# Float32 value path for four units, a fourth place for weight tiles, the first x's spread in other PSUM banks, and weight decoding queued behind its unit

## The chip, the cores and the metric

The kernel runs on one core of one Trainium2 chip. A core has five engines that run at the same time and are kept in step by semaphores: TensorE (PE in the profile, with its weight loads as PEld), VectorE (DVE), ScalarE (ACT), GpSimd (POOL) and SyncE (SP), which here issues every transfer. 16 DMA engines carry out the transfers. SBUF is the working memory and PSUM the small memory that matmuls write, in eight banks.

The metric is the device time of one execution, in microseconds (us). Each engine works off its instructions in a fixed order, one queue per engine, so an instruction that waits holds back those behind it.

## The reference

The inputs q, k and v have 4 batches, 8 heads, 768 positions and 64 columns; there are 16 centroids for each head. Every query and every key belongs to the centroid nearest in angle, and a query attends only to keys of its own cluster. The result goes through an MLP with a squared relu:

```python
q_assign = np.argmax(np.einsum('bhsd,hcd->bhsc', q_n, c_n), axis=-1)
k_assign = np.argmax(np.einsum('bhsd,hcd->bhsc', k_n, c_n), axis=-1)
mask = q_assign[:, :, :, None] == k_assign[:, :, None, :]
scores = np.where(mask, scale * np.matmul(q, k.transpose(0, 1, 3, 2)), -1e9)
attn = np.exp(scores - np.max(scores, axis=-1, keepdims=True))
attn = attn / (np.sum(attn, axis=-1, keepdims=True) + 1e-09)
x = np.matmul(attn, v).transpose(0, 2, 1, 3).reshape(B * S, H * D)
g = s * np.maximum(x @ w_in, 0.0) ** 2 + b
out = g @ w_out
```

w_in is 512 x 2048 and w_out 2048 x 512. Both lie in memory as 64-bit floats, so the kernel reads two 32-bit words for each weight and makes a float32 of them.

## The kernel before, in words

**Units.** The attention is cut into 192 units. A unit is one batch, one head and 128 queries (one of two column tiles t of a chunk of 256), against all 768 keys. They run in the order batch, chunk c (3), pair of heads hp (4), t, head h; so 16 units make one chunk of 256 rows of x, four units one pair of heads in it. A unit i passes these stages:

- `scores` (L456): four matmuls of 384 columns into a PSUM tile `sc`. The cluster mask is folded into the operands KA, KB, QA and QB, which `prep_k` and `prep_q` make from k and q: split into float16 high and low parts, transposed by DMA, matched to centroids by small matmuls (`pk`, `pq`) and a one-hot (L282).
- `maxima` (L470): a maximum over the row on DVE; `exps` (L477): a bias and the exponential on ACT, into `p`.
- `low` (L497): for the first 16 units (`TURN`) `p` is transposed on PE, in two halves e of three 128 x 128 blocks, into `turned`, one PSUM tile with two banks. For the first 8 units (`RAW`) each half is copied out as float32, half 0 by DVE and half 1 by ACT (L512, recorded at L122 and L120). For units 8 to 15 ACT copies each half as a float16 high part (L514) and DVE subtracts it to make the low part (L515). From unit 16 on the split stands before a DMA transpose (L519).
- `values` (L521): for units below 16, two at a time, the transposed weights times v. Below `RAW` that is 6 float32 matmuls a unit (L531, two records each) with v as it was loaded; else 18 float16 matmuls (L536 to L538) with the split `vh`, `vl` of v that `prep_v` makes (L407). Below `RAW` the row's sum comes from the exponential's accumulator, else from a column of ones in `vh`. From unit 16 on `value` (L551) does it in `sc`'s spare columns.
- `finish_x` (L577): after four units, the pair's part of x is split and transposed by DMA. After the fourth pair the largest value of the chunk is found across partitions by `allmax` (L94): a matmul spreads the columns, and DVE takes the maximum. `allmax` takes a one-bank PSUM tile, either of tag m or of tag h. Tag m has one buffer, which `px`, `pk`, `pq` and other spreads use in turn; tag h, also with one, belongs to the MLP's `h`.

**Weights.** The 32 weight tiles (16 of w_in, 16 of w_out, by turns) are loaded and decoded in the opening. `fetch` (L190) issues the load of one tile, 512 KB, into a stage of 4 KB per partition with three buffers (L198). `rebase` (ACT, L204) and `narrow` (two steps of DVE, L208 and L209) make the float32, and free the stage. `bound` (L212) finds the sums of absolute values, on ACT, and for w_in tiles with matmuls (L221) and a maximum on DVE (L222). After the last tile come the scales in `glob`; the column sums of w_out are spread by an `allmax` at tag m. `weights` (L228) is a generator that runs these with one tile between each two stages; three of its steps are traced before the main loop and two in each step of it (L785). When it is done, `wsplit` (L260) splits the tiles into float16 parts, on ACT (L266) and DVE (L268), one tile of each matrix from step 17 on.

**The MLP.** It has 192 steps of 256 rows x 128 hidden columns, and step m is traced with unit m + 21 (`LAG`). `mlp_start` (L602) makes the chunk's scales from the maximum of x with seven small DVE steps, `mlp_in` (L614) is 12 matmuls into `h` (L620), `mlp_relu` (L623) a relu with that scale and two squares on ACT (L627 to L630), `mlp_gl` a subtraction on POOL (L635) and `mlp_out` (L638) 6 matmuls into `acc` (L647), two steps later. `g` has four buffers of 1 KB per partition. `acc` and `turned` share one PSUM buffer of two banks (tag acc).

**The order.** The main loop (L746) traces units, MLP steps and background work step by step. The order on each engine is then made at build time, by a scheduler with a time model of its own: it issues what is ready in the model, and by priority among that. Work in a `high_priority` block is preferred; `first_of_all` (L689) gives it to the units below 20. `tc.issue_after`, wrapped as `behind` (L129), puts the instructions of a block behind a named instruction on that instruction's own engine, as an order and not as a wait. `load` puts the transfers behind the last transpose in that way.

Of the kernel before, what the change touches and what calls it, by code (L numbers as in the profile page):

```python
# [8 lines left out]
F16 = mybir.dt.float16  # L9
# [9 lines left out]
P = 128  # L19
# [7 lines left out]
def tile_cluster_attention_mlp(ctx, tc, q, k, v, cent, w_in, w_out, s_in, b_in, out):  # L27
# [15 lines left out]
    LAG = 21  # L43
    BIGN = 11

    RAW = 8
    TURN = 16
    URGENT = 20

# [43 lines left out]

    def allmax(dst, src, name, bank="m"):  # L94
        n = src.shape[1]
        pm = (ps_m if bank == "m" else ps_h).tile([P, 512], F32, tag=bank, name=f"am_{name}")
        for j in range(n):
            nc.tensor.matmul(pm[:, j * P : (j + 1) * P], src[:, j : j + 1].broadcast_to([P, P]), identb, start=True, stop=True)
        V.tensor_reduce(dst, pm[:, : n * P].rearrange("p (n q) -> p n q", q=P), axis=AX.X, op=ALU.max)
# [14 lines left out]
    G.tensor_copy(identb, ident)  # L114
    ones16 = const([P, P], F16, "ones16")
    G.memset(ones16, 1.0)

    def copy(eng, dst, src):
        if eng is A:
# [46 lines left out]
    wo = {}  # L166
    WSP = {}

    def weight_tile(name):
        return cp.tile([P, KT, P], F32, tag="w", name=name, bufs=2 * NF + 1)  # L170
    w1 = const([P, NF], F32, "w1")
# [18 lines left out]
    def fetch(p):  # L190
        ft = p // 2
        if p % 2 == 0:
            w = wi[ft] = weight_tile(f"wi{ft}")
            src = w_in.bitcast(I32)[:, ft * 2 * P : (ft + 1) * 2 * P].rearrange("(t p) f -> p t f", p=P)
        else:
            w = wo[ft] = weight_tile(f"wo{ft}")
            src = w_out.bitcast(I32)[ft * P : (ft + 1) * P, :].rearrange("p (a f) -> p a f", a=KT)
        st = sb.tile([P, KT, P, 2], I32, tag="stage", name=f"wst_{p}", bufs=3)  # L198
        load(st.rearrange("p a f w -> p a (f w)"), src)
        return {"w": w, "st": st, "p": p, "ft": ft}  # L200

# [25 lines left out]

    def weights():  # L228
        live = {}
        for i in range(2 * NF + 3):  # L230
            if 0 <= i - 3:
                bound(live[i - 3])
                narrowed[0] += 1
            if 0 <= i - 2 < 2 * NF:
                rebase(live[i - 2])
                narrow(live[i - 2])
            if i < 2 * NF:
                live[i] = fetch(i)
            if i < 2 * NF + 2:
                yield  # L240

    def finish_w_in():
# [164 lines left out]
    def prep_v(b):  # L407
        vm = sb.tile([P, 8], F32, tag="vm", name=f"vm_{b}", bufs=2)
        VM[b] = vm
        vns = []  # L410
        for hp in range(NP):
            vn = sb.tile([P, 2, T, D], F32, tag="kv", name=f"vn_{b}_{hp}", bufs=5)
            load(vn, v[b, 2 * hp : 2 * hp + 2].rearrange("h (p t) d -> p h t d", t=T), False)
            vns.append(vn)
            if b == 0:
                VN[hp] = vn
            yield
        if b:
            yield from until(START[b][3])
        for hp in range(NP):  # L420
            absmax(vm[:, hp : hp + 1], vns[hp].rearrange("p h t d -> p (h t d)"))
            if hp < NP - 1:
                yield
        vc = columns(1, f"v{b}")
        V.tensor_reduce(vc, vm[:, 0:NP], axis=AX.X, op=ALU.max)
        if b:
            yield
        allmax(vm[:, 5:6], vc, f"v{b}")
        yield
        floor2(V, vm[:, 6:7], vm[:, 5:6])  # L430
        inverse2(V, vm[:, 7:8], vm[:, 6:7], 0)
        V.tensor_scalar(vm[:, 7:8], vm[:, 7:8], 2.0 ** 13, None, op0=ALU.mult)
        V.tensor_scalar(vm[:, 6:7], vm[:, 6:7], 2.0 ** -19, None, op0=ALU.mult)
        for hp in range(NP):
            vh = sb.tile([P, 2, T, D + 2], F16, tag="vh", name=f"vh_{b}_{hp}", bufs=5)
            vl = sb.tile([P, 2, T, D], F16, tag="vl", name=f"vl_{b}_{hp}", bufs=5)
            VS[(b, hp)] = (vh, vl)
            G.memset(vh[:, :, :, D:], 1.0)
            yield from split(vh[:, :, :, :D], vl, vns[hp], vm[:, 7:8], False)
            if hp < NP - 1:  # L440
                yield
                if b > 0:
                    yield from until(48 * b - 8 + 4 * hp)
# [133 lines left out]
    def finish_x(g):  # L577
# [14 lines left out]
        if hp == NP - 1:  # L592
            xm = XM[(b, c)]
            xc = columns(1, f"x{g}")
            V.tensor_reduce(xc, xm[:, 0:NP], axis=AX.X, op=ALU.max)
            allmax(xm[:, 5:6], xc, f"x{g}")


    MS = {}
# [23 lines left out]
    def mlp_relu(b, c, ft):  # L623
# [1 line left out]
        ph = GS[(b, c, ft)]  # L625
        r = sb.tile([P, CW], F32, tag="r", name=f"r_{n}", bufs=2)
        A.activation(r, ph[:, :CW], AF.Relu, scale=MS[(b, c)][0])  # L627
        g = sb.tile([P, 2, CW], F16, tag="g", name=f"g_{n}", bufs=4)
        A.activation(g[:, 0, :], r, AF.Square)  # L629
        A.activation(r, r, AF.Square)  # L630
        GS[(b, c, ft)] = (r, g)
# [54 lines left out]
        at(LAG - 4 + ft, wsplit(ft))  # L686
    wgen = weights()

    def first_of_all(k):  # L689
        return tc.high_priority(offset=300) if k < URGENT else nullcontext()  # L690

    def run(gen):
        for _ in gen:
            pass
# [41 lines left out]
    with behind(last_turn[0], *last_split):  # L736
        some(first_v, 1)
        sv = scalar_in(s_in, "sv")
        bv = scalar_in(b_in, "bv")
        some(wgen, 3)  # L740
    run(first_k[0])
    run(first_q[0])
    run(first_k[1])
# [2 lines left out]
    while i < NU + 8 or i - LAG < NS + 4:  # L746
# [21 lines left out]
                exps(i)  # L768
        if 0 <= m < NS:
            if steps[m][2] == 0:  # L770
                mlp_start(*steps[m][:2])
            mlp_in(*steps[m])
            mlp_relu(*steps[m])
        if 0 <= i - 1 < NU:
# [38 lines left out]
```

## Time and profile before

| | |
|---|---|
| median of 3 runs | 953.33 us (951.72 to 954.87) |
| the profiled execution | 951.04 us |
| its span, from the first to the last instruction | 949.3 us |
| mean granted TensorE clock | 0.946 |
| read from HBM, written | 35.69 MB, 6.29 MB |

The profile is of one execution, and the difference between its time and its span is 1.7 us. In its 40 slices a digit is the busy share of a slice in tenths, and the granted clock in tenths of full speed. In lists of instructions, a number is the mean duration or the start, and brackets name what ended the engine's idle time. L-numbers are lines of the kernel before. A float32 matmul is recorded as two.

### The profile page before, as it was taken

What the parts mean: (1) busy time and instruction counts of PE and PEld (TensorE: products, weight loads), DVE (VectorE), ACT (ScalarE), POOL (GpSimd) and SP (SyncE); (2) the same over time, 40 slices, a digit from 0 to 9 for tenths busy, and PEclk for the clock granted to TensorE, in tenths of its full rate; (3) what the DMA queues carried; (4) which work ended last, traced back from release to release, by engine and by line L of the source; (5) the groups of instructions that cost most, each with busy time, mean ns of one, the idle gap of its engine ahead of it and who ended that gap; (6) DMA issues with size and microseconds to landing.
All of it is one profiled execution on the core that took longest, in us unless ns stands there. A gap on an engine that the chain in (4) does not pass through costs nothing. (4 is left out here: it accounts for less than half of the span.)

```text
span 949.3 us, 22900 instructions
## 1 busy us (share of the span) xinstructions
PE 835.3 (88%) x8673; PEld 586.3 (62%) x8673; DVE 639.7 (67%) x1680; ACT 713.9 (75%) x1406; POOL 546.4 (58%) x580
## 2 busy tenths in 40 slices
PE   0567566988999898999998999999999999999997
PEld 0356343656566566777676666666776667777664
DVE  7797888999577767667876766776686567654100
ACT  3476766777587777888887978887888788888443
POOL 3010114577576666778687667776776666676321
PEclk9967575899999899999999999999999999999999
DMA  6888813778787897969778877888978768575300
GB/s 174 219 215 242 225 38 78 181 141 145 160 157 146 178 200 132 181 150 180 157 173 151 198 181 147 160 146 185 180 160 167 145 129 165 125 161 114 46 23 23
DMA packets 437759, 144.25 MB, mean 152 GB/s; under 512 B 405392, under 2 KB 434064, under 8 KB 437648
## 3 DMA queue, kind: packets, MB, share of 16 engines
q1 hardware_dynamic: 437648, 142.78, 71.6%
q8 instruction: 68, 1.11, 0.5%
q14 instruction: 43, 0.35, 0.1%
HBM read 35.69 MB, written 6.29 MB: 44 GB/s over the span
## 5 line engine op out<-in xcount | busy, mean ns | idle before, releaser
L517 POOL TENSOR_TENSOR ph<-p,ph 128x768 f16<-128x768 f32 x176 | 298.5, 1696 | 92.8 <-ACT ph L120 53.8
L647 PE MATMUL acc<-wos,g 128*128 128x512 f16 x1152 | 299.8, 381 | 5.1 <-POOL g L635 4.6
L620 PE MATMUL h<-x,wis 128*128 128x256 f16 x2304 | 290.5, 275 | 5.1 <-DMA x<-xn 3.3
L620 PEld LDWEIGHTS <-wis 128*128 128x128 f16 x2304 | 220.5, 98 | 53.7 <-issue 6.7
L635 POOL TENSOR_TENSOR g<-r,g 128x256 f16<-128x256 f32 x192 | 135.0, 704 | 120.8 <-ACT r L630 100.7
L485 ACT ACTIVATE p<-sc,ssm,qsm 128x768 f32<-128x768 f32 x192 | 188.3, 981 | 2.1
L475 DVE TENSOR_REDUCE ssm<-sc 128x1 f32<-128x768 f32 x192 | 181.9, 948 | 6.9 <-PE sc L465 6.9
L647 PEld LDWEIGHTS <-g 128*128 128x128 f16 x1152 | 102.7, 98 | 82.3 <-POOL g L635 7.5
L627 ACT ACTIVATE r<-h,cf 128x256 f32<-128x256 f32 x192 | 89.6, 467 | 77.2 <-PE h L620 63.4
L120 ACT ACTIVATE ph<-p 128x768 f16<-128x768 f32 x164 | 136.4, 832 | 0.6
L482 ACT ACTIVATE ssm<-ssm,lift,qsm 128x1 f32<-128x1 f32 x192 | 73.0, 380 | 70.5 <-DVE ssm L475 68.9
L563 PE MATMUL sc<-vh,PT 128*128 128x65 f16 x1032 | 118.1, 196 | 7.0 <-DMA PT<-ph 6.8
L565 PE MATMUL sc<-vh,PT 128*128 128x65 f16 x1032 | 120.5, 194 | 0.0
L564 PE MATMUL sc<-vl,PT 128*128 128x64 f16 x1032 | 119.4, 193 | 0.0
L563 PEld LDWEIGHTS <-PT 128*128 128x128 f16 x1056 | 99.4, 98 | 26.4 <-DMA PT<-ph 13.7
L465 PE MATMUL sc<-KA,QA 128*128 128x384 f16 x384 | 99.7, 342 | 16.3 <-ACT p L485 12.8
L564 PEld LDWEIGHTS <-PT 128*128 128x128 f16 x1056 | 98.9, 100 | 12.0 <-issue 0.7
L465 PE MATMUL sc<-KB,QB 128*128 128x384 f16 x384 | 99.8, 343 | 6.2 <-DMA QB<-qb 6.2
L565 PEld LDWEIGHTS <-PT 128*128 128x128 f16 x1056 | 99.2, 98 | 1.3
L569 DVE TENSOR_SCALAR ssm<-sc 128x1 f32<-128x1 f32 x172 | 26.3, 153 | 93.8 <-PE sc L565 92.8
L629 ACT ACTIVATE g<-r 128x256 f16<-128x256 f32 x192 | 78.9, 411 | 2.7
L630 ACT ACTIVATE r<-r 128x256 f32<-128x256 f32 x192 | 78.7, 410 | 2.7
(172 smaller groups left out, 1134.7 us busy)
## 6 DMA issues: line engine op xcount, KB each, us to landing
wst<-in_moe_w_in_dram SPq DMA_DIRECT2D x16, 512.0 KB, 4.5
wst<-in_moe_w_out_dram SPq DMA_DIRECT2D x16, 512.0 KB, 4.8
kn<-in_k_dram SPq DMA_DIRECT2D x16, 384.0 KB, 3.9
qn<-in_q_dram SPq DMA_DIRECT2D x24, 256.0 KB, 3.3
vn<-in_v_dram SPq DMA_DIRECT2D x16, 384.0 KB, 4.1
out_dram<-o SPq DMA_DIRECT2D x12, 512.0 KB, 3.4
PT<-ph SPq DMA_TRANSPOSE x176, 3.4
x<-xn SPq DMA_TRANSPOSE x48, 2.7
```

The source lines that it names most:

```text
L120: A.activation(dst, src, AF.Copy)
L465: last_score[0] = nc.tensor.matmul(sc[:, e, :HALF], X[:, col, :], y[:, h * S + e * HALF : h * S + (e + 1) * HALF], start=st, stop=not st)
L475: last_max[0] = V.tensor_reduce(SM[i // 4][:, 0, j : j + 1], U[i]["sc"], axis=AX.XY, op=ALU.max, negate=True)
L485: last_exp[0] = A.activation(p.rearrange("p (a b) -> p a b", a=2), u["sc"], AF.Exp, bias=bi, scale=u["scale"], **total)
L517: G.tensor_tensor(u["ph"][:, 1, :], u["p"], u["ph"][:, 0, :], op=ALU.subtract)
L563: nc.tensor.matmul(o1, PT[:, kt, :], vh[:, h, kt, : D + 1], start=(kt == 0), stop=False)
L564: nc.tensor.matmul(o, PT[:, kt, :], vl[:, h, kt, :], start=False, stop=False)
L565: nc.tensor.matmul(o1, PT[:, T + kt, :], vh[:, h, kt, : D + 1], start=False, stop=(kt == T - 1))
L620: nc.tensor.matmul(ph[:, :CW], WSP[ft][0][:, wl, kt, :], XS[(b, c, kt)][:, :, xl, :], start=(i == 0), stop=(i == len(terms) - 1))
L627: A.activation(r, ph[:, :CW], AF.Relu, scale=MS[(b, c)][0])
L635: G.tensor_tensor(g[:, 1, :], r, g[:, 0, :], op=ALU.subtract)
L647: nc.tensor.matmul(acc[:, t, :], g[:, gl, rows], WSP[ft][1][:, wl, :], start=(ft == 0 and gl + wl == 0), stop=(ft == NF - 1 and gl == 1))
```

## The change

- `RAW` is 4 and not 8: units 4 to 7 go the float16 way of units 8 to 15. For the first batch, `prep_v` splits the pairs of heads in the order 1, 2, 3, 0, with one step between each two.
- The weight stage has a fourth place: every fourth tile (p % 4 == 3) goes into a constant tile `gs` of 4 KB per partition. Later `gs` holds the four places of `g`, which has no buffers of its own any more. `weights` fetches one tile further ahead, and four of its steps stand before the loop, with the decode of the same tile, number 0, among them.
- Rebase, narrow and bound are traced in `behind(last_exp[0], last_max[0])`: on ACT they are queued behind the exponential and on DVE behind the maximum of the unit that was traced last. Two tiles are decoded for each unit, so tiles 1 and 2 stand behind unit 0, and tile 31 behind unit 15.
- For the first chunk alone, the spread of x's maximum is written to the first bank of `turned` and not to tag m; it and `mlp_start` have high priority.

```diff
-    RAW = 8
+    RAW = 4
...
     def allmax(dst, src, name, bank="m"):
         n = src.shape[1]
-        pm = (ps_m if bank == "m" else ps_h).tile([P, 512], F32, tag=bank, name=f"am_{name}")
+        if bank == "turned":
+            pm = turned[:, 0]
+        else:
+            pm = (ps_m if bank == "m" else ps_h).tile([P, 512], F32, tag=bank, name=f"am_{name}")
...
+    gs = const([P, 4, 2, CW], F16, "gs")
...
-        st = sb.tile([P, KT, P, 2], I32, tag="stage", name=f"wst_{p}", bufs=3)
+        if p % 4 == 3:
+            st = gs.rearrange("p n e q -> p (n e q)").bitcast(I32).rearrange("p (a f w) -> p a f w", a=KT, w=2)
+        else:
+            st = sb.tile([P, KT, P, 2], I32, tag="stage", name=f"wst_{p}", bufs=3)
...
-        for i in range(2 * NF + 3):
-            if 0 <= i - 3:
-                bound(live[i - 3])
-                narrowed[0] += 1
-            if 0 <= i - 2 < 2 * NF:
-                rebase(live[i - 2])
-                narrow(live[i - 2])
+        for i in range(2 * NF + 4):
+            with behind(last_exp[0], last_max[0]):
+                if 0 <= i - 4:
+                    bound(live[i - 4])
+                    narrowed[0] += 1
+                if 0 <= i - 3 < 2 * NF:
+                    rebase(live[i - 3])
+                    narrow(live[i - 3])
             if i < 2 * NF:
                 live[i] = fetch(i)
-            if i < 2 * NF + 2:
+            if i < 2 * NF + 3:
                 yield
...
-        for hp in range(NP):
+        for hp in ((1, 2, 3, 0) if b == 0 else range(NP)):
...
-            if hp < NP - 1:
+            if b == 0 or hp < NP - 1:
                 yield
...
-            V.tensor_reduce(xc, xm[:, 0:NP], axis=AX.X, op=ALU.max)
-            allmax(xm[:, 5:6], xc, f"x{g}")
+            with first_of_all(b + c, 1):
+                V.tensor_reduce(xc, xm[:, 0:NP], axis=AX.X, op=ALU.max)
+                allmax(xm[:, 5:6], xc, f"x{g}", "m" if b + c else "turned")
...
-        g = sb.tile([P, 2, CW], F16, tag="g", name=f"g_{n}", bufs=4)
+        g = gs[:, ft % 4]
...
-        some(wgen, 3)
+        some(wgen, 4)
...
             if steps[m][2] == 0:
-                mlp_start(*steps[m][:2])
+                with first_of_all(m, 1):
+                    mlp_start(*steps[m][:2])
```

`first_of_all` is defined earlier, with the bound as an argument: `high_priority(offset=300)` if its first argument lies below the second.

More of the change, by code (lines that the diff above doesn't have):

```diff
@@ L116, in tile_cluster_attention_mlp, with first_of_all @@
     G.memset(ones16, 1.0)
+    def first_of_all(k, end=URGENT):
+        return tc.high_priority(offset=300) if k < end else nullcontext()
     def copy(eng, dst, src):
@@ L687, in tile_cluster_attention_mlp @@
     wgen = weights()
-    def first_of_all(k):
-        return tc.high_priority(offset=300) if k < URGENT else nullcontext()
     def run(gen):
```

## The prediction, made before the changed kernel was run

> **What bounds the kernel now.** I read the page first, for where the engines are less than full.
>
> ```profile
> PE 835.3 (88%) x8673; PEld 586.3 (62%) x8673; DVE 639.7 (67%) x1680; ACT 713.9 (75%) x1406; POOL 546.4 (58%) x580
> PE   0567566988999898999998999999999999999997
> PEclk9967575899999899999999999999999999999999
> ```
>
> A slice is 949.3 / 40 = 23.7 us. From the eighth slice on PE is at 8 or 9 tenths of full time and the granted clock is full; there PE sets the pace. In the first seven (0 to 166 us) PE is half idle and its clock is lowered, and everything that the change touches lies there. So the question is by how much that opening becomes shorter. The windows by stretch (columns: length, then busy us of PE, PEld, DVE, ACT, POOL with counts, clock, DMA share, GB/s) say which engine is short there:
>
> ```profile
> 96.00:108.00 12.00, 6.47 (x29) 4.20 (x29) 9.48 (x22) 10.30 (x25) 1.43 (x2) 0.50 0.73 196
> 108.00:120.00 12.00, 6.79 (x86) 5.23 (x85) 10.00 (x27) 9.07 (x20) 1.08 (x2) 0.64 0.96 256
> 156.00:168.00 12.00, 5.50 (x58) 3.42 (x59) 10.93 (x27) 7.29 (x12) 5.46 (x4) 0.50 0.49 111
> 180.00:224.00 44.00, 38.12 (x409) 25.98 (x408) 42.11 (x91) 34.47 (x68) 28.58 (x28) 0.96 0.81 161
> ```
>
> DVE is the fullest or near it in all four, never PE. In the first two, DVE stands idle for 2.5 and 2.0 us of 12, and DMA is at 0.73 and 0.96. The next view, by tile, says what it stands idle for. First the transposes of the opening's 16 units (32 halves of `turned`), then the weight stage:
>
> ```profile
> L514 ACT ACTIVATE PT<-turned x16: 468/484/492, 96.1 to 146.3; 128x384 f16<-128x384 f32 x16
> L515 DVE TENSOR_TENSOR PT<-turned,PT x16: 544/549/558, 96.6 to 147.2; 128x384 f16<-128x384 f32 x16
> L122 DVE COPY PT<-turned x8: 541/548/557, 39.0 to 86.4; 128x384 f32<-128x384 f32 x8
> L120 ACT ACTIVATE PT<-turned x8: 465/476/491, 41.5 to 89.4; 128x384 f32<-128x384 f32 x8
>   DVE PT L515: 25.5, 18
>   DVE PT L122: 12.7, 8
> ```
> ```profile
> L208 DVE TENSOR_SCALAR wi<-wi x16: 407/420/428, 26.0 to 118.9; 128x512 int32<-128x512 int32 x16
> L209 DVE SCALAR_TENSOR_TENSOR wi<-wst,wi x16: 673/683/1267, 26.9 to 119.9; 128x512 uint32<-128x512 uint32 x16
>   DMA wst<-in_moe_w_in_dram: 11.8, 11
>   DMA wst<-in_moe_w_out_dram: 8.8, 11
>   DVE wo L208: 7.2, 9
>   DVE wi L208: 4.3, 5
> ```
>
> PE sat idle 25.5 + 12.7 us before a transpose until DVE had emptied a half. ACT sat idle 11.8 + 8.8 = 20.6 us, 22 times, for a weight tile to land, and DVE behind it 7.2 + 4.3 = 11.5 us, 14 times (the last two rows). The timeline at one such place joins them (start, length, engine, line; in brackets the idle time and what ended it):
>
> ```profile
> 84.65 0.66 ACT L204 ACTIVATE wi<-wst 128x512 f32<-128x512 f32 x1 [1.75 <-DMA wst<-in_moe_w_in_dram]
> 85.34 0.43 DVE L208 TENSOR_SCALAR wi<-wi 128x512 int32<-128x512 int32 x1 [1.50 <-ACT wi L204]
> 86.41 0.55 DVE L122 COPY PT<-turned 128x384 f32<-128x384 f32 x1
> 87.01 0.90 PE L509 MATMUL turned<-ident,p 128*128 128x128 f32 x3 [3.12 <-DVE PT L122]
> 87.71 3.94 PE L531 MATMUL px<-vn,PT 128*128 128x64 f32 x18
> 91.55 0.85 PE L465 MATMUL sc<-KA,QA 128*128 128x384 f16 x2
> 93.47 1.38 PE L531 MATMUL px<-vn,PT 128*128 128x64 f32 x6
> ```
>
> A tile that lands late holds ACT, then DVE, then the copy that stood behind it, then PE: the decode is queued ahead of a unit's work and waits for a transfer. The next transpose also waits for the copy of the *other* half, so the 32 halves form one serial chain. It ends when L515 ends (last start 147.2), and only then does the first x get finished.
>
> **The weight decode and the fourth place.** Per unit two tiles are decoded. Now they stand behind that unit's exponential (ACT) and maximum (DVE), and a load starts one place earlier. The 22 waits for DMA have a mean of 20.6 / 22 = 0.94 us; a place more gives a load one tile's turn more. What those waits cost DVE is 11.5 us; the gain lies between 0 (DMA is the limit, 0.96 in 108 to 120) and 11.5. I take half, **-6**: in 96 to 108 DMA had room (0.73) while ACT and DVE waited. Next late is DVE itself, and the SP queue, which issues loads and transposes in one order.
>
> Two things are paid for it. Tiles 1 and 2, decoded now before the first scores, move behind the exponential of unit 0: 2 x (0.42 + 0.68) = 2.2 us of DVE into a fuller time; I take **+1** (0 to 2.2). And the fourth load is issued ahead of QA's transpose on SP:
>
> ```profile
> 25.39 0.67 ACT L204 ACTIVATE wo<-wst 128x512 f32<-128x512 f32 x1 [1.00 <-DMA wst<-in_moe_w_out_dram]
> 26.84 0.67 ACT L204 ACTIVATE wi<-wst 128x512 f32<-128x512 f32 x1 [0.79 <-DMA wst<-in_moe_w_in_dram]
> 27.68 1.46 PE L465 MATMUL sc<-KA,QA 128*128 128x384 f16 x4 [2.80 <-DMA QA<-qa]
> ```
>
> Tiles land 26.84 - 25.39 = 1.45 us apart and QA right after the third, so a fourth may put off the first score by 1.45; **+1** (0 to 1.45).
>
> **Four units instead of eight in float32.** Units 4 to 7 now empty each half in two steps, ACT 0.484 and then DVE 0.549, where one copy of 0.548 (DVE) or 0.476 (ACT) did. The serial chain grows by 4 x 0.484 + 4 x 0.549 = 4.1 us, 4.4 with the hand-overs, if nothing else ends later. Against it stand the value matmuls, on PE's in-order queue ahead of the next scores and transposes: 3.94 + 1.38 = 5.3 us for units 6 and 7 in float32. For a pair in float16 the first and the last of 36 are
>
> ```profile
> 111.50 0.24 PE L536 MATMUL px<-vh,PT 128*128 128x65 f16 x1 [0.30 <-DVE oe_q L288]
> 113.40 0.24 PE L538 MATMUL px<-vh,PT 128*128 128x65 f16 x1
> ```
>
> which is 2.1 us, so 3.2 less, and for both pairs at most 6.4. Net between -6.4 and +4.4; the chain is what PE waits for in the rows of `turned`, so I take **+1**. The accumulator reads and the rescaling of one x that fall away are small on ACT, which is not the limit. The new order of the splits of v (second pair first) serves unit 4's values and costs nothing while they come before them; late, the values of units 4 and 5 hold PE.
>
> [...]
>
> **The first x's spread in other banks.** The maximum over x decides the scale of the first MLP step:
>
> ```profile
> 149.94 0.16 DVE L595 TENSOR_REDUCE amb_x<-xm 128x1 bf16<-128x4 f32 x1
> 155.06 0.83 PE L620 MATMUL h<-x,wis 128*128 128x256 f16 x3
> 158.93 0.20 PE L396 MATMUL pq<-cT,QA 128*128 128x16 f16 x1 [3.04 <-DMA QA<-qa]
> 161.04 0.29 PE L98 MATMUL am_x<-identb,amb_x 128*128 128x128 bf16 x1 [1.52 <-DVE oe_q L288]
> 165.35 0.45 ACT L627 ACTIVATE r<-h,cf 128x256 f32<-128x256 f32 x1
> 168.21 2.11 PE L620 MATMUL h<-x,wis 128*128 128x256 f16 x9
> ```
>
> The input of the spread is ready at 150.1, but it runs at 161.0: it shares bank m with `pq`, which waits for QA to land. In the banks of `turned`, free since 147.8, and ahead of other work, it runs at about 150.3. Then the last three h matmuls (155.06 to 155.9) end last, and the first relu starts at about 156.0 in place of 165.35: 9.4 us earlier; the next h, now at 168.21, follows. Of these 9.4 us only what PE and DVE can fill is gained. From 156 to 168 PE has 12.00 - 5.50 = 6.5 us free, DVE only 1.1, and from 180 to 224 DVE is busy 42.11 of 44. I take **-5.5** (0 to -9.4): splits of weights are made ahead, so the first steps need little of DVE. The high priority of the few small DVE steps costs nothing beside this.
>
> `gs` lends its space to every fourth weight tile and is then the four places of g, as many as before, so MLP steps are spaced as before.
>
> **Sum.** -6 + 1 + 1 + 1 - 5.5 = -8.5 from the profiled execution's 951.04 (span 949.3) gives 942.5. The median of the runs, 953.33, lies 2.3 above that execution: **945**. With all good ends, -11.5 - 6.4 - 9.4 = -27.3, it is 926; with all bad ones, +4.4 + 2.2 + 1.45 = +8, it is 961.
>
> **Rivals.**
>
> - *Only the bank pays.* Loads come no faster (0.96 of DMA is already used in 108 to 120), the decode waits move. -5.5 + 3 = -2.5: 950.8, at the bound of what can be told. For it: that row. Against it: 0.73 in 96 to 108. Chance 0.15.
> - *DVE takes it all back.* What starts earlier waits for the splits of weights until 224, where DVE is busy 42.11 of 44. 953. Against it: DVE's idle time before 120 is real room. Chance 0.11.
> - [...] Chance 0.05.
> - *Slower: the weights become last.* The last two tiles may now be decoded only after unit 15's exponential.
>
> ```profile
> 123.93 0.17 DVE L252 TENSOR_REDUCE amb_w<-l 128x1 bf16<-128x16 f32 x1
> 130.33 0.28 DVE L99 TENSOR_REDUCE glob<-am_w 128x1 f32<-128x128 f32 x1
> 131.44 0.99 ACT L485 ACTIVATE p<-sc,ssm,qsm 128x768 f32<-128x768 f32 x1
> ```
>
> If the decode waits do not shrink, the chain's 4.4 and the moved tiles' 2.2 stand alone, and that exponential (131.44) comes at about 138. The weights are then ready two decodes (some 3 us) and the bounds' spread (130.33 - 123.93 = 6.4 us) later, at 147, and only then can their splits begin, in DVE's fullest stretch: the MLP waits for splits and the bank's -5.5 is lost. That gives +4.4 + 2.2, 960. It decides from the point where x follows unit 15's exponential by less than about 9.4 us and the few splits of the first steps; now it is 155.06 - 131.44 = 23.6, and this distance speaks against it. Chance 0.14.
> - A false dependency in `gs`, or an order of the whole program that comes out worse: slower, 0.03.
>
> **How the numbers follow.** The forecast has 0.52; its own range is 936 to 950. About 0.3% (2.9 us, so 950.5 to 956.2) is what a measurement can tell here. Faster: 0.50 of the forecast, 0.05 for the overlap and 0.08 of the first rival, 0.63; same: 0.02, 0.07 and 0.10 of the second rival, 0.19; slower: 0.14, 0.03 and 0.01, 0.18. The range 931 to 959 takes in all but the outer ends of the sum.
>
> **What would show it.** Right: am_x within 1 us of its input, the first relu 10 us or more earlier than 165.35; waits of ACT for `wst` well under 20.6 us; L531 with 48 records, L515 with 24, and unit 15's exponential earlier than 131.44. Wrong: L595 later than 150, waits for `turned` above 40 us in all, or the same start of the MLP with DVE full up to 224. If the MLP starts earlier by far more than the run gets shorter, the gain was eaten on DVE between 150 and 230.

## The result and the profile after

The changed kernel takes 962.76 us (median of 4 runs, 961.06 to 965.67) where the kernel before took 953.27 us beside it (4 runs, 951.72 to 954.87): a ratio of 1.0106, with a 95% interval of 1.0072 to 1.0140. The profiled execution took 961.06 us, with a span of 959.4 us. The forecast was 945, in a range of 931 to 959; the result is slower than the whole range. The ratio, here and below, is estimated from the single runs and not from the two medians, whose quotient can differ from it by up to 0.3%. One later run, of a shifted kernel before (before_p64), took 1249 us at a granted clock of 0.65, and its ratio leaves that run out.

The lines below answer to those that the prediction shows of the kernel before. Line numbers are now those of the changed kernel, some 12 higher. First the page:

```profile
PE 827.6 (86%) x8697; PEld 578.0 (60%) x8697; DVE 639.1 (67%) x1684; ACT 715.0 (75%) x1405; POOL 551.7 (58%) x580
PE   0565567876999989999999989899998999999997
PEclk9976577999999999999999999999999999999999
```

The totals are the same to 1.4%. In the row of PE, slices 8 to 10 (168 to 240 us) read 8, 7, 6 where before had 9, 8, 8. Further down slices 24, 26 and 31 have an 8 for a 9, as slices 14, 16 and 22 have in before. Next the same stretches of the opening:

```profile
96.00:108.00 12.00, 6.25 (x34) 4.01 (x32) 9.15 (x20) 8.08 (x18) 1.69 (x2) 0.50 0.46 138
108.00:120.00 12.00, 7.17 (x63) 5.00 (x62) 8.07 (x19) 7.88 (x15) 1.12 (x2) 0.51 0.79 199
156.00:168.00 12.00, 9.92 (x85) 6.64 (x85) 10.13 (x20) 6.86 (x14) 5.07 (x5) 0.66 0.49 67
180.00:224.00 44.00, 33.70 (x374) 22.02 (x371) 38.75 (x89) 33.27 (x63) 27.70 (x23) 1.00 0.83 174
```

The stretch behind them (before, then after):

```profile
224.00:248.00 24.00, 21.06 (x226) 14.20 (x225) 18.91 (x55) 17.21 (x35) 18.67 (x18) 1.00 0.80 139
```
```profile
224.00:248.00 24.00, 15.76 (x160) 10.15 (x159) 22.47 (x57) 14.97 (x30) 16.18 (x13) 0.93 0.57 120
```

DMA moves less between 96 and 120 us than before (138 and 199 GB/s, against 196 and 256), and DVE is less full, not fuller. From 180 to 224 us, where DVE had 42.11 of 44 us, it has 38.75, and PE 33.70 instead of 38.12. So up to 224 us nothing in these rows became a bound by being full; work arrives late. From 224 to 248 us, where the last splits of weights now stand, DVE is fuller than before (22.47 of 24 us against 18.91), and PE has 15.76 instead of 21.06. The waits at `turned` and at the weight stage (by tile; microseconds and times that an engine sat idle until that was done):

```profile
L526 ACT ACTIVATE PT<-turned x24: 462/490/505, 70.1 to 147.7; 128x384 f16<-128x384 f32 x24
L527 DVE TENSOR_TENSOR PT<-turned,PT x24: 541/550/558, 72.9 to 150.7; 128x384 f16<-128x384 f32 x24
  DVE PT L527: 42.5, 28
  DVE PT L128: 1.2, 2
```
```profile
L215 ACT ACTIVATE wi<-wst x16: 649/666/685, 23.6 to 130.6; 128x512 f32<-128x512 f32 x16
  DMA wst<-in_moe_w_in_dram: 6.3, 5
```

ACT's waits for a weight tile fell from 20.6 to 6.3 us, and 0.5 us at the tiles in `gs`, as the prediction asked for. But the decode of the last w_in tile starts at 130.6 where it started before 119, and the waits at `turned` rose from 38.2 to 43.7 us. The timeline shows what the decode waits for instead:

```profile
135.29 0.98 ACT L497 ACTIVATE p<-sc,ssm,qsm 128x768 f32<-128x768 f32 x1
136.69 0.66 ACT L215 ACTIVATE wo<-gs 128x512 f32<-128x512 f32 x1
139.90 0.16 DVE L264 TENSOR_REDUCE amb_w<-l 128x1 bf16<-128x16 f32 x1
140.68 0.28 DVE L102 TENSOR_REDUCE glob<-am_w 128x1 f32<-128x128 f32 x1
142.83 1.32 DVE L280 SCALAR_TENSOR_TENSOR wis<-wi,glob,wis 128x512 f16<-128x512 f32 x1
153.09 0.16 DVE L608 TENSOR_REDUCE amb_x<-xm 128x1 bf16<-128x4 f32 x1
153.70 0.31 PE L101 MATMUL turned<-identb,amb_x 128*128 128x128 bf16 x1
160.53 0.46 ACT L640 ACTIVATE r<-h,cf 128x256 f32<-128x256 f32 x1
```

The first row is unit 15's exponential, 3.9 us later than before. The last tile is decoded 1.4 us behind it, because the queueing puts it behind that unit; in the kernel before that happened at 120.8, ten microseconds ahead of the exponential. The first split of a weight follows at 142.8 (before: 125.3), and the last at 243.3 (before: 224.3). The spread of x's maximum runs 0.6 us after its input, as intended, and the first relu comes at 160.5: 4.8 us earlier, not 9.4.

None of that is left at the third chunk. Its scale, which needs the x of that chunk and which its MLP needs first, is made at the same time in both kernels (before, then after):

```profile
323.22 0.20 DVE L609 TENSOR_SCALAR cf<-xm,glob 128x1 f32<-128x1 f32 x1
```
```profile
323.24 0.21 DVE L622 TENSOR_SCALAR cf<-xm,glob 128x1 f32<-128x1 f32 x1
```

The end comes 10.0 us later all the same. From about 346 us on, both kernels have every instruction in the same order on every engine, and yet one stage differs. It runs from the scale of the sixth chunk to that of the eighth (columns as in the windows above; before, then after):

```profile
523.20:653.10 129.90, 124.58 (x1375) 87.55 (x1372) 89.03 (x247) 106.51 (x210) 89.37 (x88) 1.00 0.84 171
```
```profile
525.50:663.00 137.50, 124.95 (x1374) 87.64 (x1371) 87.82 (x247) 106.33 (x210) 89.02 (x88) 1.00 0.80 162
```

The work of every engine is the same to 1.4%, the clock is full in both, and the stage is 7.6 us longer. What PE waits for in it (times in total, how often, the longest; before, then after):

```profile
PE sc L465 <- ACT p L485: 2.3, 4, 1.1
PE acc L647 <- POOL g L635: 1.1, 3, 0.5
PE pq L396 <- DMA QA<-qa: 0.2, 1, 0.2
```
```profile
PE pq L408 <- DMA QA<-qa: 3.5, 2, 2.4
PE sc L477 <- ACT p L497: 3.1, 5, 1.0
PE acc L660 <- POOL gs L648: 2.2, 2, 1.1
```

Transfers land later, and PE waits for them or for what stands behind them. The experiments had to explain two things: what the opening loses, and why a stage with the same instructions in the same order takes 7.6 us more.

### The profile page after: what moved, and what is told of

Same layout as the page of the kernel before. It is cut to its first block, busy times and chain, and to the rows that moved or that the text cites. A ratio compares the mean times of both kernels' runs of the same rounds, so it can differ in the third digit from the quotient of the medians.

```text
span 959.4 us, 22945 instructions
## 1 busy us (share of the span) xinstructions
PE 827.6 (86%) x8697; PEld 578.0 (60%) x8697; DVE 639.1 (67%) x1684; ACT 715.0 (75%) x1405; POOL 551.7 (58%) x580
## 3 DMA queue, kind: packets, MB, share of 16 engines
q8 instruction: 68, 1.11, 0.5%
## 5 line engine op out<-in xcount | busy, mean ns | idle before, releaser
L660 PE MATMUL acc<-wos,gs 128*128 128x512 f16 x1152 | 298.2, 379 | 7.9 <-POOL gs L648 6.2
L648 POOL TENSOR_TENSOR gs<-r,gs 128x256 f16<-128x256 f32 x192 | 138.6, 722 | 118.5 <-ACT r L643 95.1
L660 PEld LDWEIGHTS <-gs 128*128 128x128 f16 x1152 | 101.4, 97 | 83.3 <-POOL gs L648 9.2
L642 ACT ACTIVATE gs<-r 128x256 f16<-128x256 f32 x192 | 78.9, 411 | 2.7
```

The source lines that it names most:

```text
L648: G.tensor_tensor(g[:, 1, :], r, g[:, 0, :], op=ALU.subtract)
L660: nc.tensor.matmul(acc[:, t, :], g[:, gl, rows], WSP[ft][1][:, wl, :], start=(ft == 0 and gl + wl == 0), stop=(ft == NF - 1 and gl == 1))
```

## Experiments on the parts

The theories at this point: A, the queued decode makes the splits late, and this costs the run. B, the rival for the late stage: `g` now lies in another place of memory, and this slows later transfers. C: the late stage depends on when transfers fall, which the opening decides. A part "alone" is added to the kernel before, "without" means the change less that part. Ratios are to the kernel before in the same session, with 95% intervals.

**The change once more, unaltered** (after_again).

> The changed kernel once more, unaltered. In its first profile the third chunk's scale (cf) stands at 323.2 us, the same as before, the sixth at +2.3, the eighth at +9.9. Theory A (the opening: weights decoded 16 us later make the splits late) expects the whole difference to lie ahead of 323 and the 8 us between 525 and 665 to be chance of one execution: gone or elsewhere in this profile, and a time of 953 to 957. Theory B (a lasting effect on transfers in the later part, where both kernels have the same order of instructions) expects the same 8 us in the same stretch and 961 to 965.

Measured: 961.38 us (two runs, 956.36 and 966.39 us), 1.0110 (1.0034 to 1.0186); in the one of 966.39, which was profiled, the late stage takes 139.5 us. The loss repeats, in the same stage.

**The queueing alone** (beh_only).

```diff
         for i in range(2 * NF + 3):
-            if 0 <= i - 3:
-                bound(live[i - 3])
...
+            with behind(last_exp[0], last_max[0]):
+                if 0 <= i - 3:
+                    bound(live[i - 3])
...
```

> Only the decode queued behind the unit's exponential and maximum; float32 for eight units, three places, bank m. Theory A: the last tile is decoded at 135 us or later, the last split at 240 or later, and the time is 957 to 964, most of the change's loss. Theory B: 951 to 955, for the memory is laid out as before.

Measured: 948.81 us, 0.9968 (0.9944 to 0.9991). The splits are late here too (last one at 239.4), and the kernel is a little faster, below what A and B expected. Theory A, as a theory of the whole loss, does not survive this alone.

**All but the queueing** (no_beh: `weights` without `behind`, the rest of the change).

> The change without the queueing of the decode. Theory A: the last tile before 125 us, the last split before 225, the first relu near 156 by the bank, and a time of 945 to 950. Theory B: 959 to 964, since gs lies where it lay in the change.

Measured: 946.93 us, 0.9954 (0.9938 to 0.9970). The last tile is decoded at 108.5, the first relu comes at 148.5, the scale of the third chunk at 315.1.

**The fourth place alone** (gs_only).

```diff
-        st = sb.tile([P, KT, P, 2], I32, tag="stage", name=f"wst_{p}", bufs=3)
+        if p % 4 == 3:
+            st = gs.rearrange("p n e q -> p (n e q)").bitcast(I32).rearrange("p (a f w) -> p a f w", a=KT, w=2)
+        else:
+            st = sb.tile([P, KT, P, 2], I32, tag="stage", name=f"wst_{p}", bufs=3)
...
-        g = sb.tile([P, 2, CW], F16, tag="g", name=f"g_{n}", bufs=4)
+        g = gs[:, ft % 4]
...
-        some(wgen, 3)
+        some(wgen, 4)
```

> Only the fourth place in gs, which later holds g. Theory A: loads earlier by one place, the last tile 2 to 5 us earlier than 122 us, time 948 to 953. Theory B (the new place of tiles in memory slows later transfers): 958 to 963, with the loss after 500 us.

Measured: 948.73 us, 0.9965 (0.9943 to 0.9988); the last tile is decoded at 108.8, 12 us earlier than before where A had 2 to 5, and the scale of the third chunk comes at 313.2, 10.0 us earlier than before. At the end of the span 2.7 us of that are left.

**The memory place of g alone** (g_const).

```diff
+    gs = const([P, 4, 2, CW], F16, "gs")
...
-        g = sb.tile([P, 2, CW], F16, tag="g", name=f"g_{n}", bufs=4)
+        g = gs[:, ft % 4]
```

> The kernel before with g held in the constant tile gs, and nothing else: the weight stage keeps three places. Every engine has the same instructions in the same order as before; only places in memory and the way g's places are released differ. Theory B (the place of tiles in memory costs the changed kernel 8 to 13 us late): 958 to 963, with the loss after 500 us. Theory C (the late loss comes from when the transfers of the later part fall, which the opening decides): 950 to 954, the same as before.

Measured: 951.90 us, 0.9993 (0.9972 to 1.0015), the late stage 129.9 us. Theory B is out.

**All but the fourth place, and all but the float32 part** (no_gs: three stage buffers and `g` in buffers of its own; no_raw: `RAW = 8` and the old order of the splits of v).

> The change without the fourth place: float32 for four units, decode behind its unit, bank of turned. The order of the later part is that of before and of the change. Theory B: 948 to 953, no loss after 500 us, as in the kernel with the queueing alone (948.8). Theory C: cannot be told in advance, but if the loss is there (959 or more) theory B is out.

> The change with float32 for eight units again. The order of the later part is that of before and of the change. Theory A (splits late): as the change, for the decode is queued as there: relu 16 to 28 some 5 to 8 us later than before. Theory B: 958 to 963. If float32 for four units is what costs: 948 to 953.

Measured: no_gs 955.02 us, 1.0004 (0.9977 to 1.0031), with 137.7 us in the late stage; no_raw 951.64 us, 0.9983 (0.9959 to 1.0008), with 129.8.

**Queueing and fourth place together** (beh_gs: the edits of beh_only and gs_only).

> Fourth place and queueing together, without the float32 part and the bank. Each of the two alone was 3 us faster than before (948.7 and 948.8). If the two hurt each other in the opening (four places, but a decode that is held back): first split after 140 us and 957 to 962. If they do not: 944 to 949.

Measured: 962.76 us, 0.8 us above the range given for two parts that hurt each other, 1.0078 (1.0049 to 1.0107). Each of the two alone is faster than before; together they are slower. The opening alone shows the same: the scale of the third chunk comes at 317.2 us with the queueing, at 313.2 with the fourth place, and at 327.0 with both (before: 323.2).

Leaving out any one of three parts seemed to cure the loss, and neither of the two that ran alone made it (the float32 part and the bank did not run alone). But one thing was regular: among the kernels with the late order of before, the late stage took 129.4 to 129.9 us with `RAW = 8` (before, beh_only, g_const, no_raw), and 137.5 to 139.5 us with `RAW = 4` (after, after_again, no_gs), though the float32 way ends at 150 us. Theory C did not give that: no_gs and no_raw have quite different openings from after and before.

## Experiments on the place of the program's pieces

What differs at 525 us between these two groups? One load shows it. It is q's, issued at the same point of the program in both; the view of DMA gives, for the time from its issue until it has landed, the packets of each queue and the load's own time (before, then after):

```profile
q1 hardware_dynamic: 1912, 0.61, 77.6%
qn<-in_q_dram SPq DMA_DIRECT2D x1, 256.0 KB, 3.1
```
```profile
q1 hardware_dynamic: 2426, 0.73, 71.5%
q8 instruction: 1, 0.02, 2.2%
qn<-in_q_dram SPq DMA_DIRECT2D x1, 256.0 KB, 4.4
```

In the changed kernel a packet of "q8 instruction" falls into the load's time, and the load takes 4.4 us, not 3.1. DVE, which waits for it, is 1.24 us later from there on. The page says what this queue carries in the whole run:

```profile
q8 instruction: 68, 1.11, 0.5%
```

68 packets, 1.11 MB: 16 KB each. PE has 17,482 records in this trace (8,697 matmuls, as many weight loads, 88 of its sequencer), 17,482 / 68 = 257 for each packet. The packets begin 127.4 matmuls apart on the mean, which with as many weight loads and 88 / 68 = 1.3 records of the sequencer is 256. So I take them for PE's own program, fetched while it runs in pieces of 256 instructions: an estimate from these counts.

In all 20 traces of this case together, between 330 and 840 us, I sorted the transposes of `ph` by whether a piece's fetch begins 0.5 to 2.5 us after their issue: 340 with a fetch have a median of 4.79 us from issue to landing. 1,114 have no packet of q8, nor of q14, the other queue of that kind (43 packets, 0.35 MB), from 2 us before to 3 us after their issue, and a median of 3.29. For the loads of q it is 4.01 against 3.12 (40 and 166), for the transposes of x 4.06 against 2.54 (132 and 249). A fetch itself takes 0.9 to 2.6 us, with a median of 1.08.

This gives theory D: a transfer that meets a fetch lands 0.9 to 1.5 us later, and which transfers meet one is decided by the number of instructions that PE has had. `RAW = 4` has 24 more matmuls and weight loads than `RAW = 8`, and 6 instructions of the sequencer less: 42 of 256. Counted in matmuls from the end of the run, the last 48 pieces of the changed kernel begin 18 sooner on the mean than those of the kernel before (42 instructions are 21 matmuls with their weight loads).

The experiment shifts the pieces and nothing else. Idle matmuls of one column go ahead of everything on PE; all other instructions keep their order on all engines:

```diff
     G.memset(ones16, 1.0)
+    pad = ps_m.tile([P, 512], F32, tag="m", name="pad")
+    for _ in range(21):
+        nc.tensor.matmul(pad[:1, :1], ones[:, :1], ones[:, :1], start=True, stop=True)
```

They lie where PE has nothing to do. The timeline of the kernel before with 21 of them:

```profile
1.58 0.67 PE L119 MATMUL pad<-ones 128*1 128x1 bf16 x21 [1.58 <-POOL ones L109]
5.42 0.29 PE L98 MATMUL am_k<-identb,amb_k 128*128 128x128 bf16 x1 [3.17 <-DVE cs L152]
```

**Before with 21, the change with 107** (before_p21, after_p107: 107 are 214 instructions, and 42 + 214 = 256, one whole piece).

> The kernel before with 21 more matmuls of one column ahead of everything on PE, where PE waits for its first input anyway; every other instruction stands in the old order on all engines. 21 matmuls with their weight loads are 42 instructions, as many as PE's program has more in the changed kernel. Theory D (a transfer lands about 1.3 us later when PE's next piece of program, 16 KB or 256 instructions, is fetched beside it, and the number of instructions decides which transfers are hit): the stage from the sixth to the eighth chunk's scale takes 137 to 139.5 us as in the changed kernel, not 129.9, and the kernel 958 to 963 us. Theory A (the late loss comes from the later splits of weights and what follows from them): nothing of that is in this kernel, 952 to 954 us, stage 129.9.

> The changed kernel with 107 such matmuls ahead, 214 instructions, so that the pieces of PE's program begin where they began in the kernel before (42 + 214 = 256); the order of all else is that of the changed kernel. Theory D: the stage from the sixth to the eighth chunk's scale is back at 130 us from 137.5, and the time at 951 to 955 us, no slower than before. Theory A: the splits come as late as in the changed kernel, so 961 to 964 us and a stage of 137 to 139.

Measured: before_p21 962.51 us, 1.0103 (1.0077 to 1.0129); after_p107 955.45 us, 1.0040 (1.0017 to 1.0063). The late stage of before_p21, then of after_p107:

```profile
525.10:664.10 139.00, 126.44 (x1376) 88.14 (x1373) 88.51 (x247) 106.44 (x210) 88.58 (x88) 0.99 0.81 161
```
```profile
524.70:654.70 130.00, 124.61 (x1375) 87.56 (x1372) 88.85 (x248) 106.44 (x210) 89.06 (x88) 1.00 0.84 171
```

The last 48 pieces begin 20 matmuls sooner than in the kernel before in before_p21, and within one of it in after_p107. 21 idle matmuls, done 3 us before PE is needed, make the kernel before as slow as the changed one, and 107 take the late loss out of the changed one. In before_p21 PE waits 3.5 us for QA in this stage, as in the change; in after_p107 it waits 0.2, as in the kernel before. Theory D holds; A, which expected 952 to 954 and 961 to 964, does not. after_p107 missed its expectation by half a microsecond: it is not level with before, but 0.4% slower.

**Half a piece** (before_p64, after_p64: 64 idle matmuls, 128 instructions).

> The kernel before with 64 matmuls ahead, 128 instructions, half a piece of PE's program. Theory D: other transfers are hit than in both kernels; the stages' lengths change by several us each, the total lies anywhere from 943 to 965 us, not within 1 us of the kernel before in each stage. Theory A: 952 to 954 us and every stage as before within 1 us.

> The changed kernel with 64 matmuls ahead, 128 instructions. Theory D: the stages from 325 us on differ from those of the changed kernel by several us each, though no order differs; the total anywhere from 943 to 968 us. Theory A: 961 to 964 us, every stage as in the changed kernel within 1 us.

Measured: before_p64 957.36 us, 1.0048 (1.0020 to 1.0076), late stage 136.2 us; after_p64 957.92 us, 1.0066 (1.0042 to 1.0091), late stage 132.9. As D has it, the stages move by several microseconds with no other change.

**The version without the float32 part, shifted by 21** (no_raw_p21).

> The change without the float32 part (no_raw, which took 951.64 us, 0.9983 of before), and 21 idle matmuls of one column ahead on PE, so that PE's program has 42 instructions more again; nothing else moves. Theory D (place of the program's pieces): the stage from the sixth to the eighth chunk's scale goes from 129.8 to 137 to 139.5 us and the time to 958 to 964. Theory E (float32 for units 4 to 7 itself saves the kernel from the late loss): 951 to 953 us, stage 129.8.

Measured: 957.24 us, 1.0059 (1.0036 to 1.0082), 0.8 us under the range given; the late stage:

```profile
521.40:658.80 137.40, 124.80 (x1376) 87.69 (x1372) 88.60 (x248) 106.69 (x210) 88.71 (x88) 1.00 0.78 162
```

129.8 has become 137.4. Leaving out the float32 part had cured the late stage by moving the pieces, not by its own work.

**The change without the queueing, at two other places** (no_beh_p107, no_beh_p64).

> The change without the queueing (no_beh, 946.93 us, 0.9954 of before), with 107 idle matmuls, so that the pieces of PE's program begin where they do in the kernel before and in after_p107. Theory F (queueing the decode behind the exponential and the maximum costs the opening 6 us or more by itself, at an equal place of the pieces): 944 to 950 us, that is 0.992 to 0.998, at least 5 us under after_p107 with its 955.45 us. Theory G (the whole difference between the change and no_beh is the place of the pieces): 953 to 957 us, as after_p107.

> The change without the queueing, with 64 idle matmuls (half a piece further than no_beh). Theory F: the scale of the third chunk's MLP stays at 315 us as in no_beh, the stages after it move by some us each way, 940 to 955 us in all. Theory G: as far from no_beh as after_p64 is from the change, so 943 us.

Measured: no_beh_p107 950.08 us, 0.9972 (0.9951 to 0.9993); no_beh_p64 948.93 us, 0.9964 (0.9943 to 0.9984). The pieces of no_beh_p107 and after_p107 begin at nearly the same place, so their difference of 0.7% is the queueing: F holds (0.1 us above its range of times), and G falls, as it does with no_beh_p64, where it gave 943. There the scale of the third chunk comes at 317.0 us, 1.9 later than in no_beh. The change and the same without the queueing can be compared at two more nearly equal places in the table below: 74 and 69 (1.0106 against 0.9954) and 203 and 198 (1.0066 against 0.9964). At all three the queueing costs the change, 0.7, 1.5 and 1.0%, and it delays the scale of the third chunk by 7.4, 8.1 and 6.5 us. The weight tiles that go through `gs` (no_beh_p107, then after_p107):

```profile
L218 ACT ACTIVATE wo<-gs x8: 649/656/675, 27.8 to 108.3; 128x512 f32<-128x512 f32 x8
```
```profile
L218 ACT ACTIVATE wo<-gs x8: 648/662/671, 43.3 to 136.5; 128x512 f32<-128x512 f32 x8
```

With the queueing the first of them is decoded 15.5 us later and the last 28.2 us later; the scale of the third chunk comes at 322.2 instead of 314.8.

**The fourth place alone, at three other places** (gs_only_p64, then gs_only_p32 and gs_only_p96).

> The kernel before with the fourth place for weight tiles alone (gs_only, 948.73 us, 0.9965 of before), with 64 idle matmuls ahead. If the gain of the fourth place is made in the opening, the scale of the third chunk stays at 313 us and the rest moves with the place of the pieces, 940 to 958 us; if gs_only was only lucky in that place, the scale of the third chunk goes back to 320 us or more and the time to 953 or above.

> The fourth place alone with 32 idle matmuls ahead, a quarter of a piece of PE's program; with none it took 948.73 us (0.9965), with 64 it took 942.45 us (0.9897). Theory D: up to the scale of the third chunk (313 us) it is as those two within 2 us, and the stages after it differ again; the total lies anywhere from 940 to 955 us. The other theory, that the idle matmuls themselves help (they warm PE up, or shift the start): 942 to 944 us, since any number of them would do.

> The fourth place alone with 96 idle matmuls ahead, three quarters of a piece. Theory D: the scale of the third chunk at 312 to 315 us, the total anywhere from 940 to 955 us and not the same as with 32 and 64. The other theory, that idle matmuls themselves help: 942 to 944 us.

Measured: gs_only_p64 942.45 us, 0.9897 (0.9866 to 0.9928); gs_only_p32 945.65 us, 0.9923 (0.9905 to 0.9941); gs_only_p96 948.42 us, 0.9953 (0.9936 to 0.9969). In all four the scale of the third chunk comes at 312 to 315 us, against 323.2 before: the gain of the opening is real, and how much of it is left at the end depends on the place. Idle matmuls as such do not help, since 96 give less than 64. gs_only_p64 is the fastest version of the study, 1.0% faster than the kernel before and 2.1% faster than the change.

All versions by the place of their pieces (PE's records in the trace, modulo 256), with the time of the third chunk's scale and the time that PE sits idle from there to the end, both from the profiled execution:

| place | version | ratio | third scale, us | PE idle after it, us |
|---|---|---|---|---|
| 20 | fourth place alone | 0.9965 | 313.2 | 30.0 |
| 22 | fourth place and queueing | 1.0078 | 327.0 | 31.4 |
| 26 | queueing alone | 0.9968 | 317.2 | 22.6 |
| 26 | fourth place, queueing and bank (no_raw) | 0.9983 | 320.8 | 24.0 |
| 28 | all but the queueing (no_beh_p107) | 0.9972 | 314.8 | 29.4 |
| 32 | before | 1 | 323.2 | 22.6 |
| 32 | memory place of g alone (g_const) | 0.9993 | 322.6 | 23.7 |
| 33 | the change (after_p107) | 1.0040 | 322.2 | 25.9 |
| 69 | fourth place, queueing and bank (no_raw_p21) | 1.0059 | 318.8 | 31.2 |
| 69 | all but the queueing | 0.9954 | 315.1 | 27.8 |
| 69 | all but the fourth place | 1.0004 | 315.1 | 32.9 |
| 74 | the change as it is | 1.0106 | 323.2 | 30.9 |
| 74 | the change once more | 1.0110 | 321.5 | 34.9 |
| 75 | before (before_p21) | 1.0103 | 323.3 | 33.8 |
| 85 | fourth place alone (p32) | 0.9923 | 312.1 | 26.4 |
| 149 | fourth place alone (p64) | 0.9897 | 312.3 | 24.6 |
| 161 | before (before_p64) | 1.0048 | 321.9 | 28.3 |
| 198 | all but the queueing (no_beh_p64) | 0.9964 | 317.0 | 27.7 |
| 203 | the change (after_p64) | 1.0066 | 323.5 | 28.7 |
| 213 | fourth place alone (p96) | 0.9953 | 315.2 | 29.1 |

One order of one program spans 0.2 to 1.0% over the two to four places tried (all but the queueing: 0.9954 to 0.9972; the fourth place alone: 0.9897 to 0.9965; before: 1 to 1.0103). The last two columns split the loss of 10 us in the span. Up to the third chunk's scale the change takes as long as before. Behind it PE has nearly the same work left (605.2 us against 603.5), and sits idle for 30.9 us and not 22.6. The kernel before stands by luck at a good place: of all versions only the queueing alone idles as little there, and before itself idles for 33.8 and 28.3 us at its two other places.

## Why the prediction was wrong

It gave -8.5 us; the change costs +9.5 (962.76 - 953.27). Two things failed: the -6 for the weight decode and the fourth place, which had 0 as its worst end, and the sentence that everything the change touches lies in the first 166 us. Read at nearly equal places (20 to 33), the table gives the terms, each the step from one version to the next, times 952 us, the time of before beside most of these runs. Two ratios with their intervals stand behind each step, so each is uncertain by 2 to 4 us.

- **The fourth place.** Alone -3.3 us (0.9965), and -6.2 as the mean of its four places (0.99345) against before at its one good place; against the mean of before's three places (1.0050) it is -11. The weights are decoded 12 us earlier and the scale of the third chunk comes 8 to 11 us earlier. For this half of the step the direction of the -6 was right; its size depends on the places compared.
- **The queueing: this step failed.** The prediction put it into the same -6, as though a decode that stands behind an exponential only lost its waits. On top of the fourth place it costs 0.9965 to 1.0078, +10.8 us, and in the whole change 0.9972 to 1.0040, +6.5. ACT's waits for transfers did fall from 20.6 to 6.8 us, because the tiles now wait in their places: from landing to the start of its decode a tile waits 5.1 us on the mean, where it waited 0.2. The decode was held back to two tiles for each unit, up to unit 15. Waits that vanish were counted as a gain; they had only changed their name. This is in part the mechanism of the rival "the weights become last": the last decode (136.7) stands behind unit 15's exponential (expected at 138, measured at 135.3), and the splits come from 142.8 on (expected from 147). Its condition, that the waits do not shrink, did not hold, and PE waits for splits in the first steps of the MLP for 3.6 us only. Of the three signs that the prediction named for wrong, two came up: x's maximum has its input at 153.1, later than 150, and the waits at `turned` exceed 40 us. The rival gave 960, that is +6.6 us; with the pieces placed as before the change costs +3.8, so its time came near the result with the help of a cause that it did not contain.
- **Why the two hurt each other is not shown.** The queueing alone has the same ties and late splits, and is not slower. Unit 15's exponential starts at 131.4 us in before, at 126.5 with the fourth place alone, 128.5 with the queueing alone, 132.3 with both; in the change at 135.3, without the queueing at 125.4, without the fourth place at 126.9. A landed tile waits 4.6 and 5.1 us for its decode where both are there, and 1.7 us or less in the other five. That a place gains nothing when the step that empties it is tied to something later fits these waits; it does not say why the units themselves fall behind.
- **The first score** comes at 28.93 instead of 27.68, as the +1 for the fourth load ahead of QA's transpose had it.
- **The float32 part.** no_raw to after_p107 is +5.4 us, and at the other place (no_raw_p21 to after) +4.5. The serial chain of `turned` was worked out at 4.4, and unit 15's exponential is 3.7 us later (131.4 in no_raw, 135.1 in after_p107). The +1 had set half of the saved value matmuls against this. The rows show them gone (48 records instead of 96), and no gain from them in the queued versions. Without the queueing, float32 part and bank together cost 0.7 us (gs_only to no_beh_p107).
- **The bank.** beh_gs to no_raw is -9.0 us, where -5.5 was taken and -9.4 was the end. In the opening this is -6.2 us (the scale of the third chunk, 327.0 to 320.8). The rest is PE's idle time behind it, 31.4 to 24.0: there the order of the program changes too, so the -9.0 is not the bank's price alone. Beside the float32 part and without the queueing, the first relu comes 13.4 us earlier (161.7 in gs_only, 148.3 in no_beh_p107), and the scale of the third chunk 1.6 us later: nothing of it lasts. As the prediction has it, only what PE and DVE can fill is gained; without the queueing that was next to nothing.
- **A term that no step had: the place of the pieces.** after_p107 to after is +6.3 us of the +9.5. The prediction counted 24 more matmuls on PE by their time. That PE's program is fetched in pieces could be seen in the trace of before (68 packets of instructions), and the prediction did not use it.
- **The sum:** -3.3 + 10.8 - 9.0 + 5.4 + 6.3 = +10.2. It meets the +9.5 to +10.5 measured because each term starts where the last one ends, so it is no check of the terms.
- **The overlap of the halves**, which has 0.05 of the chances and the 4.4 us behind them, is a term that no run shows. In the traces of before and after, no transpose into `turned` runs while DVE or ACT reads a half out (0 of 24.7 and of 29.0 us of reading), and PE waits 42.5 us for the DVE step at L527, 25.5 for the same step before.
- **A loose reading without consequence:** the prediction calls the granted clock full from the eighth slice on; its own row has 8 tenths in slices 8 and 14.

**What stays open.** The queueing costs only beside the fourth place, and alone it was measured at one place. Which single transfer decides the late stage was not followed: QA's wait is 3.3 of the 7.6 us, the rest spreads. The versions of the fourth place lose 1.6 to 7.3 us of their lead between the third chunk and the end, by place. From about 350 us on the 20 traces have only two orders of instructions: that of before, in 12 of them, and another, in those with the fourth place alone, without the queueing, and with both. PE sits idle behind the third chunk's scale for 28.3 us on the mean with either. So neither order is slower as such. But an equal place does not mean equal hits in two orders: at places 20 to 33 the one idles for 22.6 to 25.9 us, the other for 29.4 to 31.4, and the steps between them (the fourth place, the bank) hold this difference. And why a transfer that meets a fetch lands later is not shown: the delays of 0.9 to 1.5 us are of the size of a fetch (0.9 to 2.6 us), but the trace here doesn't tell on which DMA engine a packet ran.

## What to carry to other kernels

A tighter order ("behind that instruction") and a further buffer can each pay and together cost (here 0.9968 and 0.9965 alone, 1.0078 together). Look for when the last of the queue is done, and how long a landed tile waits, not only at how the waits of the engine shrink. Before a difference of about 1% is put down to an edit, compare each version at several places of its program pieces, by idle instructions ahead on the engine whose fetches the trace shows (here PE, 68 packets). Counts that agree modulo 256 were enough here only where the order behind them was the same too (at places 20 to 33 PE idled for 22.6 to 25.9 us in one order, 29.4 to 31.4 in the other). And the number itself can be tuned: 64 idle matmuls made the best version 0.7% faster at no cost.

## What was unexpected of the hardware

Every 14 us on the mean (68 times in 959 us), a 16 KB piece of PE's program is fetched by DMA beside the kernel's own transfers, and a transfer that meets it lands 0.9 to 1.5 us later on the median (PT 3.29 to 4.79 us, x 2.54 to 4.06, q 3.12 to 4.01). In this kernel, whose transposes go through DMA, this moved a stage of 130 us by up to 9 us (129.9 in before, 139.0 in before_p21) with not one instruction in another order.
